# Block 0's first product: wider matmuls for tile pairs, and tile 3 prepared one step sooner

## The chip, the cores and the metric

One core of a Trainium2 chip runs the kernel. The metric is the device time of one execution in microseconds (us); lower is better. Every time below is of the kernel before the change.

## What is computed

Linear attention without a softmax for 8 batches of 8 heads, a norm per head, then a layer norm and a two-layer network with a residual:

```python
kv  = einsum('bhsd,bhse->bhde', k, v)          # q, k, v: (8, 8, 576, 64)
out = einsum('bhsd,bhde->bhse', q, kv)
out = out / sqrt(mean(out*out, -1) + 1e-6) * g_norm
x   = out.transpose(0, 2, 1, 3).reshape(8, 576, 512)
xn  = (x - mean(x)) / sqrt(var(x) + 1e-6) * g_ln
y   = x + maximum(xn @ w_ch1, 0) @ w_ch2       # w_ch1: 512 x 2048, w_ch2: 2048 x 512
```

## The kernel before

**Blocks and tiles.** Each batch gives a block of 512 rows, in four tiles of 128 rows; the 64 rows left of each batch make a ninth block, "rem". Per tile the kernel makes the attention output (`o`), its squares (`sq`, ScalarE), their sums per head (`red`, VectorE), the root of these (`root`, ScalarE, L383), then on VectorE the scaled rows (`y`, L379, and `x`, L397) and the centred, weighted rows in bf16 (`xc`, L407). `turn` transposes these on TensorE (L429) into PSUM, and ScalarE copies them into `xT_blk` (L431), the right operand of the first product.

**First product.** `mm1(b, t0, n, c0, c1)` multiplies tiles t0 to t0+n-1 by the column blocks c0 to c1 of w1 (16 of 128 columns each). One step fills one PSUM bank with 4/n column blocks of n tiles: 16 matmuls 128 columns wide for n = 1, 8 matmuls 256 wide for n = 2, 4 accumulations (`kk`) for each column block. ScalarE then reads the bank in one relu (L678) into `m1`. The banks come from the pool `ps1`, which has three. In blocks 2 to 8 the steps take two or four tiles at once; in blocks 0 and 1 one.

**Second product.** `mm2_part` (L697) multiplies `m1` by w2. For block 0 it starts when all of `mm1(0, ...)` is issued, on two `ps1` and two `ps2` banks.

**Order of the work.** It is written by hand. Each engine runs its instructions in the order in which they are issued. Ahead of each step `mm1` calls `tick()`, which first issues what `at(slot, fn)` has put down for that step, in order of the slot: `at(5.1, before_5)` comes in step 5, behind `at(5, ...)`. Block 0's first product is steps 0 to 15, its second product steps 16 and up. The steps of the kernel before:

| step | products of block 0 | issued ahead of them |
|---|---|---|
| 0 | tile 0, c 0 to 4 | |
| 1 | tile 1, c 0 to 4 | `before_1`: tile 1's transpose, tile 2's `o`, `sq`, `red`, `root`, tile 0's `x_g` |
| 2 | tile 0, c 4 to 8 | `before_2`: tile 2's `o_g`, `x_g`, `xc`; tile 1's `x_g` |
| 3 | tile 1, c 4 to 8 | |
| 4 | tile 0, c 8 to 12 | |
| 5 | tile 1, c 8 to 12 | tile 2's `turn`; `before_5`: all of tile 3 up to `xc` |
| 6 to 8 | tile 2, c 0 to 12 | |
| 9, 10 | tiles 0 and 1, c 12 to 16 | memsets and the loads of batch 2 at step 9 |
| 11 | tile 2, c 12 to 16 | tile 3's `turn` |
| 12 to 15 | tile 3, c 0 to 16 | `q_start` at step 14 |

In block 0 the tiles' `o` have banks of their own: tile 1's in `ps1`, tile 2's in `ps_m`, tile 3's in `ps2` (two banks). `x_g` is the variant of `x` for tiles 0 to 2, which reads a second attention product (`og_ps`) that already holds g_norm.

**Loads.** w1 comes in four pieces of four column blocks (`load_w1`, L115) on POOL's queue, one behind the other, then pieces of w2 (L119) among the loads of batch 1.

Of the kernel before, what the change touches and what calls it, by code (L numbers as in the profile page):

```python
# [14 lines left out]
def kernel(  # L15
# [84 lines left out]
    def load_batches(slot, what, after):  # L100

        def start(i, name, b):
            if i == 0:
                for element in after():
                    nc.gpsimd.tensor_copy(gate, element)
            dst, src = {"k": (k_in, k), "v": (v_in, v), "q": (q_in, q)}[name]
            load(dst[b % NB], src, b)

        for i, (name, b) in enumerate(what):
            at(slot[i] if isinstance(slot, tuple) else slot, lambda i=i, name=name, b=b: start(i, name, b))  # L110
# [325 lines left out]
    def main_tile(b, j, pool=None, tag="ops"):  # L436
        q_t, kvp = qts[b], held[b]
        if b not in blks:
            blks[b] = new_block()
        return Tile([(slice(0, 128), lambda hp: q_t[:, j, hp, :], kvp)], blks[b], j, pool, tag)  # L440
# [32 lines left out]
    def m1_of(b):  # L473
        if b not in m1s:
            m1s[b] = m1pool.tile([128, nDe, 512], bf16, tag="m1", name="m1")
        return m1s[b]
# [22 lines left out]
    def row_sums(b, i0, i1, ticks):  # L499
        if b not in sums:  # L500
            sums[b] = [spool.tile([128, H2, 256], bf16, tag=f"S{i}", name=f"S{i}")
                       for i in (1, 2, 4)]
            sums[b].insert(2, m1_q(b, 1, 0))
        s = slice(i0, i1)
        S1, S2, S3, S4 = (t[:, s] for t in sums[b])
        a11, a12, a21, a22 = (m1_q(b, r, o)[:, s] for r, o in ((0, 0), (0, 1), (1, 0), (1, 1)))
        for i, fn in enumerate((lambda: nc.vector.tensor_add(S1, a21, a22),  # L507
                                lambda: nc.vector.tensor_sub(S2, S1, a11),  # L508
                                lambda: nc.vector.tensor_sub(S4, a12, S2),  # L509
                                lambda: nc.vector.tensor_sub(S3, a11, a21))):  # L510
            agenda.setdefault(clock[0] + ticks[i], []).append((-1, fn))
# [153 lines left out]
    def mm1(b, t0, n, c0=0, c1=nDe):  # L665
        blk, m1 = blks[b], m1_of(b)
        sl = slice(t0 * 128, (t0 + n) * 128)
        per = 4 // n
        for de0 in range(c0, c1, per):
            tick()  # L670
            p1 = ps1.tile([128, per, n * 128], f32, tag="p1", name="p1")
            for i in range(per):
                de = de0 + i
                for kk in range(nK):
                    nc.tensor.matmul(p1[:, i, :], lhsT=w1_sb[:, kk, de * 128:(de + 1) * 128],  # L675
                                     rhs=blk[2][:, kk, sl],
                                     start=(kk == 0), stop=(kk == nK - 1))
            nc.scalar.activation(m1[:, de0:de0 + per, sl], p1, func=AF.Relu)  # L678
            del p1
            if b == 2 and t0 + n == 4 and de0 + per in SPLIT_2:  # L680
                i = SPLIT_2.index(de0 + per)
                row_sums(b, SPLIT_2[i - 1] // 2, SPLIT_2[i] // 2, TICKS_2[i - 1])
            elif b in SEVEN and b != 2 and de0 + 1 in SPLIT:
                i = SPLIT.index(de0 + 1)
                row_sums(b, SPLIT[i - 1] // 2, SPLIT[i] // 2, range(4))
# [62 lines left out]
    def at(slot, fn):  # L748

        i, r = divmod(slot, 32)  # L750
        blocks = [*range(B), "rem"]
        if r > 16 and i < len(blocks) and blocks[int(i)] in SEVEN:
            r = 16 + (r - 16) * 14 / 16
        s = sum(30 if x in SEVEN else 32 for x in blocks[:int(i)]) + r
        agenda.setdefault(int(s + 1e-6), []).append((s, fn))

    def tick():
        for _, fn in sorted(agenda.pop(clock[0], []), key=lambda e: e[0]):
            fn()
        clock[0] += 1  # L760
# [15 lines left out]
    t = [main_tile(0, 0)] + [main_tile(0, i, *((ps1, "p1"), (ps_m, "misc"), (ps2, "p2"))[i - 1])  # L776
                             for i in range(1, 4)]
# [77 lines left out]
        t[2].xc()  # L855
        t[1].x_g()

    def before_5():
        t[3].o()
        t[3].sq()  # L860
        t[3].red()
        t[3].y()
        t[3].x()
        t[3].xc()
# [7 lines left out]
    at(1, before_1)  # L872
    at(2, before_2)
    at(5, lambda: t[2].turn(True))
    at(5.1, before_5)
    at(9.5, next_memsets)
    load_batches(9.6, (("k", 2), ("v", 2), ("q", 2)), lambda: ())
    at(11, lambda: t[3].turn(True))
    for i in range(4):
        at(16 + i, lambda i=i: t[i].var())  # L880
    at(20, lambda: (rstd_of(0), t.clear()))
# [73 lines left out]
        at(40 + i, fn)  # L955


    for ts, c0, c1 in ((0, 0, 4), (1, 0, 4), (0, 4, 8), (1, 4, 8), (0, 8, 12), (1, 8, 12),
                       (2, 0, 12), (0, 12, 16), (1, 12, 16), (2, 12, 16), (3, 0, 16)):
        mm1(0, ts, 1, c0, c1)  # L960
    p2s = [ps1.tile([128, Dm], f32, tag="p1", name="p2") for _ in range(2)]
    p2s += [ps2.tile([128, Dm], f32, tag="p2", name="p2") for _ in range(2)]
    for de0, de1 in ((0, 8), (8, 10), (10, 12)):
# [50 lines left out]
```

## Time and profile before

| | |
|---|---|
| three runs | 279.30, 279.38, 279.63 us; median 279.38 |
| the profiled execution | 279.33 us, of which the span is 277.3 |
| granted TensorE clock | 1.00 |
| TensorE busy | 269.2 us, 97% of the span |
| VectorE, ScalarE, POOL busy | 71%, 65%, 37% |
| block 0's first product | 14.83 to about 32.4 us |

The span is the time from the first to the last instruction; the execution's time has some 2 us more around it. PE is TensorE's matmuls, PEld its weight loads, one for each matmul here, DVE is VectorE, ACT is ScalarE. A share of busy time says how full an engine is on average, not what a stage waits for; an end of a matmul in the profile is modelled, so starts are safer to count from. A wait is put down to what ended last ahead of it; "issue" is time for which the profile shows no releaser.

### The profile page before, as it was taken

The page shows a single profiled execution, that of the slowest core. Times are in us where ns is not written, and L with a number is a line of the kernel's source. Part 1 is how long each engine was busy: PE and PEld are TensorE (multiplying, and loading weights), DVE is VectorE, ACT ScalarE, POOL GpSimd, SP SyncE. Part 2 cuts the span into 40 slices and gives each one's busy share as a digit, 9 for nine tenths or more (in the row PEclk, how much of TensorE's full clock was granted, in tenths as well). Part 3 has the DMA queues.
Part 4 walks back from the last instruction along what each step waited for, and adds up shares of the span by engine and source line. Part 5 has one row for each costly group of instructions (what it writes and reads, how often), then busy time and mean ns, then how long its engine had stood idle before and what let it go on. Part 6 is the DMA issues. An engine that isn't in the chain of part 4 may idle for free.

```text
span 277.3 us, 6629 instructions
## 1 busy us (share of the span) xinstructions
PE 269.2 (97%) x2614; PEld 189.6 (68%) x2614; DVE 195.9 (71%) x446; ACT 179.5 (65%) x398; POOL 101.7 (37%) x127
## 2 busy tenths in 40 slices
PE   8899999999999999999999999999999999999994
PEld 3589855996569886458845874597458745874683
DVE  6676438897966898899569856985797469923564
ACT  3567754796448783777677767776777487846610
POOL 8522770025034256701870187017201800180141
PEclk9999999999999999999999999999999999999999
DMA  7999999959995994995499639991611061105032
GB/s 215 199 207 205 200 197 190 260 106 144 189 183 84 199 126 92 216 227 98 41 185 239 134 26 178 245 134 21 161 28 21 20 163 29 21 20 151 2 76 76
DMA packets 65366, 36.80 MB, mean 133 GB/s; under 512 B 35120, under 2 KB 62004, under 8 KB 65336
## 3 DMA queue, kind: packets, MB, share of 16 engines
q0 software_dynamic: 28736, 18.29, 46.4%
q1 hardware_dynamic: 36008, 17.12, 30.4%
q10 hardware_dynamic: 592, 0.98, 1.0%
q8 instruction: 20, 0.33, 0.5%
q14 instruction: 10, 0.08, 0.1%
HBM read 36.71 MB, written 9.44 MB: 166 GB/s over the span
## 4 chain that ended last, share of the span: by engine, by line
PE 82%; DVE 8%; DMA 4%; ACT 3%; issue 1%; POOL 1%; DVEq 0%; POOLq 0%
PE p L675 42%; PE p L697 8%; PE p_y L519 7%; PE p_z L519 7%; PE p_x L519 6%; PE p_s L519 4%; DMA w_sb<-in_moe_w_ch_dram 4%; PE p_q L519 3%; PE o_ps L298 2%; PE kv_ps L271 2%; DVE S L509 1%; DVE ss L375 1%; DVE x_blk L397 1%; DVE o_ps L379 1%; DVE S L508 1%
## 5 line engine op out<-in xcount | busy, mean ns | idle before, releaser
L675 PE MATMUL p<-xT_blk,w_sb 128*128 128x128 bf16 (+2 forms) x1024 | 131.5, 286 | 0.6 <-DMA w_sb<-in_moe_w_ch_dram 0.4
L678 ACT ACTIVATE m<-p 128x512 bf16<-128x512 f32 x144 | 85.5, 597 | 38.9 <-PE p L675 36.2
L675 PEld LDWEIGHTS <-w_sb 128*128 128x128 bf16 x1024 | 78.7, 98 | 45.0 <-issue 0.7
L519 PEld LDWEIGHTS <-m 128*128 128x128 bf16 x448 | 43.3, 98 | 6.5
L375 DVE TENSOR_REDUCE ss<-sq 128x8 f32<-128x512 f32 x35 | 23.8, 680 | 28.7 <-ACT sq L304 28.6
L582 POOL TENSOR_TENSOR q<-q,x_blk 128x512 f32<-128x512 f32 x6 | 8.1, 1348 | 83.1 <-ACT q L553 83.1
L519 PEld LDWEIGHTS <-S 128*128 128x128 bf16 x344 | 32.8, 98 | 4.8 <-DVE S L509 1.1
L697 PE MATMUL p<-w_sb,m 128*128 128x512 bf16 x128 | 29.6, 379 | 0.0
L415 ACT ACTIVATE dev<-x_blk,st_blk 128x512 f32<-128x512 f32 x36 | 25.8, 718 | 1.4 <-DVE st_blk L401 1.4
L379 DVE TENSOR_TENSOR o_ps<-o_ps,inv 128x512 f32<-128x512 f32 x33 | 23.1, 700 | 3.1
L304 ACT ACTIVATE sq<-o_ps 128x512 f32<-128x512 f32 x35 | 20.8, 595 | 5.0 <-PE o_ps L298 5.0
L397 DVE SCALAR_TENSOR_TENSOR x_blk<-o_ps,g_norm_sb 128x512 f32<-128x512 f32 x33 | 22.8, 691 | 1.1
L519 PE MATMUL p_x<-w_sb,m 128*128 128x256 bf16 x192 | 23.4, 273 | 0.0
L697 PEld LDWEIGHTS <-m 128*128 128x128 bf16 x128 | 12.0, 98 | 12.3
L383 ACT ACTIVATE rms<-ss,eps_sb 128x8 f32<-128x8 f32 x36 | 10.7, 297 | 12.6 <-DVE ss L375 12.2
L507 DVE TENSOR_TENSOR S<-m 128x768 bf16<-128x768 bf16 (+2 forms) x20 | 10.7, 536 | 11.4 <-ACT m L678 11.4
L422 DVE TENSOR_SCALAR xc<-x_blk,st_blk 128x512 bf16<-128x512 f32 x32 | 17.7, 553 | 1.1
L558 DVE SCALAR_TENSOR_TENSOR u<-p_y,rstd,v 128x256 f32<-128x256 f32 x24 | 10.4, 476 | 5.0 <-PE p_y L519 5.0
L509 DVE TENSOR_TENSOR S<-m,S 128x768 bf16<-128x768 bf16 (+2 forms) x20 | 12.6, 634 | 0.4
L553 ACT ACTIVATE v<-p_x,rstd 128x256 f32<-128x256 f32 x24 | 9.4, 475 | 5.0 <-PE p_x L519 5.0
L390 DVE RECIPROCAL inv<-rms 128x8 f32<-128x8 f32 x36 | 7.1, 197 | 7.6 <-ACT rms L383 7.3
L519 PE MATMUL p_z<-w_sb,S 128*128 128x256 bf16 x96 | 11.8, 273 | 0.6 <-DVE S L509 0.6
(143 smaller groups left out, 347.6 us busy)
## 6 DMA issues: line engine op xcount, KB each, us to landing
out_dram<-o_sb SPq DMA_DIRECT2D x24, 256.0 KB, 6.1
w_sb<-in_moe_w_ch_dram POOLq DMA_DIRECT2D x7, 512.0 KB, 13.5
q_in<-in_q_dram POOLq DMA_DIRECT2D x7, 320.0 KB, 5.2
k_in<-in_k_dram POOLq DMA_DIRECT2D x7, 320.0 KB, 7.8
v_in<-in_v_dram POOLq DMA_DIRECT2D x7, 320.0 KB, 11.1
q_in<-in_q_dram POOLq DMA_DIRECT2D x8, 256.0 KB, 8.2
out_dram<-o_sb SPq DMA_DIRECT2D x16, 128.0 KB, 4.6
k_in<-in_k_dram POOLq DMA_DIRECT2D x7, 256.0 KB, 8.7
```

The lines of the kernel that those rows point to most:

```text
L304: nc.scalar.activation(self.sq_t, self.o_ps, func=AF.Square)
L375: nc.vector.tensor_reduce(self.ss, self.sq_t, axis=AX.X, op=ALU.add)
L379: nc.vector.tensor_mul(self.o_ps, self.o_ps, self.inv().to_broadcast([128, H, D]))
L383: nc.scalar.activation(self.r, self.ss, func=AF.Sqrt, scale=1.0 / D, bias=eps_sb)
L397: nc.vector.scalar_tensor_tensor(x_blk[:, ts].rearrange("p (h d) -> p h d", h=H), in0=self.o_ps, scalar=1.0, in1=g_norm_sb.to_broadcast([1 ...
L415: nc.scalar.activation(dev, x_blk[:, ts], func=AF.Square, bias=st[:, 1, ts:ts + 1], accum_out=st[:, 2, ts:ts + 1])
L422: nc.vector.tensor_scalar_add(self.xc_t, x_blk[:, self.ts], st[:, 1, self.ts:self.ts + 1])
L509: lambda: nc.vector.tensor_sub(S4, a12, S2),
L519: nc.tensor.matmul(dst[:, t - ts[0], :c1 - c0], lhsT=a[:, i, t * 128:(t + 1) * 128], rhs=w[:, i, c0:c1], start=start and t == ts[0] and i ...
L675: nc.tensor.matmul(p1[:, i, :], lhsT=w1_sb[:, kk, de * 128:(de + 1) * 128], rhs=blk[2][:, kk, sl], start=(kk == 0), stop=(kk == nK - 1))
L678: nc.scalar.activation(m1[:, de0:de0 + per, sl], p1, func=AF.Relu)
L697: nc.tensor.matmul(p2[:, c0:c1], lhsT=m1s[b][:, de, ts * 128:(ts + 1) * 128], rhs=w2_sb[:, de, c0:c1], start=(de == 0), stop=(de == nDe - 1))
```

## The change

The step list of block 0's first product is regrouped. Tiles 0 and 1 are still taken one by one for c 0 to 4, then together (n = 2) for c 4 to 12 and for c 12 to 16; tiles 2 and 3 are taken together for c 12 to 16. The steps stay 16: tile 0 (step 0), tile 1 (1), tiles 0 and 1 (2 to 5), tile 2 (6 to 8), tiles 0 and 1 (9, 10), tile 3 (11 to 13), tiles 2 and 3 (14, 15). Tile 3's `o`, `sq` and `red` are issued at step 4, not 5, and its `turn` at step 10, not 11.

```diff
-    def before_5():
+    def before_4():
         t[3].o()
         t[3].sq()
         t[3].red()
+
+    def before_5():
         t[3].y()
         t[3].x()
         t[3].xc()
...
     at(5, lambda: t[2].turn(True))
+    at(4, before_4)
     at(5.1, before_5)
     at(9.5, next_memsets)
     load_batches(9.6, (("k", 2), ("v", 2), ("q", 2)), lambda: ())
-    at(11, lambda: t[3].turn(True))
+    at(10, lambda: t[3].turn(True))
...
-    for ts, c0, c1 in ((0, 0, 4), (1, 0, 4), (0, 4, 8), (1, 4, 8), (0, 8, 12), (1, 8, 12),
-                       (2, 0, 12), (0, 12, 16), (1, 12, 16), (2, 12, 16), (3, 0, 16)):
-        mm1(0, ts, 1, c0, c1)
+    for ts, n, c0, c1 in ((0, 1, 0, 4), (1, 1, 0, 4), (0, 2, 4, 12), (2, 1, 0, 12), (0, 2, 12, 16),
+                          (3, 1, 0, 12), (2, 2, 12, 16)):
+        mm1(0, ts, n, c0, c1)
```

## The prediction

> **What bounds the kernel now.** I read the page first, for which engine sets the span. Its columns are busy time, share of the span, count; in the groups, busy and mean ns, then idle time before them and who ended it.
>
> ```profile
> span 277.3 us, 6629 instructions
> PE 269.2 (97%) x2614; PEld 189.6 (68%) x2614; DVE 195.9 (71%) x446; ACT 179.5 (65%) x398; POOL 101.7 (37%) x127
> ...
> L675 PE MATMUL p<-xT_blk,w_sb 128*128 128x128 bf16 (+2 forms) x1024 | 131.5, 286 | 0.6 <-DMA w_sb<-in_moe_w_ch_dram 0.4
> ```
>
> TensorE is the bound, and the groups show almost no idle time ahead of the first products. But a busy matmul is a modelled length that covers the next one's start, so small waits hide in it. The timeline of the weight loads (start, length, count), which come one per matmul, shows them; here block 0's first product:
>
> ```profile
> 18.68 2.80 PEld L675 LDWEIGHTS <-w_sb 128*128 128x128 bf16 x48
> 21.45 0.27 PEld L429 LDWEIGHTS <-xc 128*128 128x128 bf16 x4
> 21.67 0.27 PEld L298 LDWEIGHTS <-qt 128*128 128x128 bf16 x4
> 21.89 2.78 PEld L675 LDWEIGHTS <-w_sb 128*128 128x128 bf16 x49
> 24.87 2.66 PEld L675 LDWEIGHTS <-w_sb 128*128 128x128 bf16 x47 [0.20 <-issue]
> 27.49 0.26 PEld L429 LDWEIGHTS <-xc 128*128 128x128 bf16 x4
> 27.71 0.99 PEld L675 LDWEIGHTS <-w_sb 128*128 128x128 bf16 x17
> 28.87 3.56 PEld L675 LDWEIGHTS <-w_sb 128*128 128x128 bf16 x63 [0.17 <-issue]
> 32.38 0.58 PEld L697 LDWEIGHTS <-m 128*128 128x128 bf16 x4
> ```
>
> From 24.87 to 27.49 there are 47 loads: 55.7 ns each, 0.892 us per step of 16. At that pace the 49 from 21.89 would end at 24.62, not 24.87: 0.25 us lost after the first load of step 8 (49 = 3 x 16 + 1). The 17 from 27.71 would end at 28.66, not 28.87: 0.21 us lost at the start of tile 3, step 12. These are the two waits that the change can touch. A third, of 0.09, lies in the first line (2.77 us for 48 loads, 2.67 at the pace): step 3 goes on when ScalarE's relu of step 1 (19.09 to 19.67) has ended, which the change leaves alone.
>
> Who is waited for: ScalarE's timeline.
>
> ```profile
> 20.81 0.60 ACT L678 ACTIVATE m<-p 128x512 bf16<-128x512 f32 x1 [0.38 <-PE p L675]
> 21.70 0.60 ACT L678 ACTIVATE m<-p 128x512 bf16<-128x512 f32 x1 [0.30 <-PE p L675]
> 22.20 0.58 ACT L431 COPY xT_blk<-tp 128x512 bf16<-128x512 bf16 x1
> 22.66 0.61 ACT L304 ACTIVATE sq<-o_ps 128x512 f32<-128x512 f32 x1
> 24.03 0.30 ACT L383 ACTIVATE rms<-ss,eps_sb 128x8 f32<-128x8 f32 x1 [0.75 <-DVE ss L375]
> 24.24 1.55 ACT L678 ACTIVATE m<-p 128x512 bf16<-128x512 f32 x3
> ...
> 28.24 0.58 ACT L431 COPY xT_blk<-tp 128x512 bf16<-128x512 bf16 x1
> ```
>
> Tile 3's root (L383) stands in ScalarE's order ahead of step 5's relu (L678) and waits 0.75 us for VectorE's sum, which waits for the square at 22.66. Three relus pile up behind it, and step 8 waits for the bank that the first of them gives back near 24.84. At 28.24 the copy of tile 3's transpose ends at 28.82; step 12 goes on at 28.87.
>
> **Wider products.** 64 pairs of 128-column matmuls become 64 of 256 columns: 32 pairs in steps 2 to 5, 16 in steps 9 and 10, 16 in steps 14 and 15. The columns stay the same; only what a matmul costs beyond its columns is saved. Block 2's first product has the wide form, in TensorE's timeline:
>
> ```profile
> 82.25 3.66 PE L675 MATMUL p<-xT_blk,w_sb 128*128 128x256 bf16 x32
> 85.74 0.39 PE L298 MATMUL o_ps<-kv_pack,qt 128*128 128x128 bf16 x4
> ```
>
> 3.49 us for 32 is 109.1 ns, against 2 x 55.7 = 111.5. Saved: 64 x 2.4 ns = 0.15 us, all on the bounding engine. The 64 weight loads that go too were hidden (98 ns each, started every 55.7). The Trainium skill, "TensorE: Matmul & The Clock Gate", section "Back-to-back issue gap", gives about 81 ns for each 128-column matmul in a stream of load and matmul pairs, and 131 ns for 512 columns; interpolated, an estimate from that page, 256 columns would cost some 98 ns and the term would be 64 x 64 ns = 4.1 us. The trace does not agree: 55.7 ns in this very stage.
>
> There are still 16 steps, and each fills one bank that one relu of 512 columns reads (597 ns), so ScalarE's work and every later entry of the agenda keep their step. The second w1 piece is first used at step 2, the third at 4, the last at 9, as before. The step-4 load at 20.56 goes out as the third piece lands (POOL, waiting for that semaphore, goes on at 20.81), so that coming earlier would gain nothing; 0.22 us of tile 3's matmuls now stand ahead of it. Tile 1 is needed from step 1 on in both.
>
> **Tile 3 made a step sooner.** Three instructions move from step 5 to step 4: `o` (4 matmuls on TensorE, ahead of step 4's products), `sq` (ScalarE, ahead of step 4's relu and tile 2's copy) and `red` (VectorE, after tile 1's `x_g`, in the same order as before). No DMA moves, and nothing passes POOL's or SP's queue. I play it through with the rows' spacings (a relu starts 0.25 us after its step's last load, as 21.45 to 21.70; a full ScalarE operation holds its queue 0.50, as 21.70 to 22.20).
>
> Step 3 ends at 20.53 instead of 20.56. `o` loads from 20.53 to 20.75; step 4's eight wide ones end at 21.62; tile 2's transpose at 21.84; step 5 at 22.72, where step 6 wants tile 2's columns. ScalarE: step 3's relu 20.78, `sq` 21.28 to 21.89, step 4's relu 21.87, tile 2's copy 22.37 to 22.95. Before, that copy ended at 22.78, just as step 6 began. So step 6 goes on at 23.0 instead of 22.78: **a new wait of 0.22 us**. Queued behind it is all of TensorE.
>
> In return the sum runs on VectorE at 21.94 (it is free of `x_g` at 21.85 by its timeline) to 22.63; the root comes at 22.83 and waits for nothing, step 5's relu at 23.04 instead of 24.24, and **step 8's wait of 0.25 us goes**. What is late next is tile 2's copy, above.
>
> Tile 3's `xc` ends 3.05 us after its root (24.03 to 27.08 before), so at 25.88. Its transpose, now at step 10, is wanted at about 26.49: covered by 0.6 us. The copy then ends at 27.82, and step 11 goes on at 27.87, wanted at 27.64: 0.23 lost, against 0.21 now. That wait only moves.
>
> **Sum**, against the profiled execution (span 277.3, time 279.33; the 2.0 us around the span stay): -0.15 - 0.25 + 0.22 + 0.02 = -0.16 us, so the second product starts at about 32.22 instead of 32.38. The rest follows TensorE: the next waits (`kv_ps` at 52.73, about 0.2 us; `p_z` at 105.47, 0.58 us idle by TensorE's timeline) are ScalarE's and VectorE's, behind work that TensorE starts, and shift along. The DMA-bound row nearest is VectorE's `q_p` copy at 55.11; tile 3 of block 1, made after it, is ready at 58.30 and transposed at 59.08, so 0.16 us fits into that 0.78. 279.33 - 0.16 = 279.17; the runs' median is 0.05 higher, so **279.2 us**. What a measurement can tell from no change is about 0.2%, 0.56 us (the three runs spread over 0.33): the forecast is no measurable change.
>
> The unknown cost is the new wait at step 6. At best the copy is out before step 6 (as now): 0, sum -0.38. At worst every ScalarE operation holds its queue for its full 0.60: relu 20.78, `sq` 21.38, relu 21.98, copy 22.58 to 23.16, wait 0.43, sum +0.05. I take 0.22, by the spacing of the rows just there.
>
> **Rivals.**
>
> *Both copies come in time.* If step 6 finds tile 2 ready and step 11 finds tile 3 ready, then -0.15 - 0.25 - 0.21 = -0.61 us: 278.8. For: the copy at 22.20 was just in time. Against: one more full operation is ahead of tile 2's copy, and tile 3's is in the same place as at 28.24. Chance 0.20.
>
> *The wide form saves more*, by the 81 ns rule: 275.3. Against: the pace of the loads above. Chance 0.02.
>
> *The gain is given back*: a later product waits for VectorE or a transfer whose time stands still. 279.4, in the margin. Against: the margins above. Chance 0.10.
>
> *Slower: `o` waits for its bank.* Tile 3's `o` writes a bank of the two-bank pool `ps2`, which the turned q of tile 3 (`tp`) and tile 2's `og_ps` held. The trace shows the last readers ending at 18.60 (ScalarE, L846) and 20.22 (VectorE, L365), and only that at 21.67 the load went out unhindered. If the bank is given back later than the readers show, all of TensorE stands from 20.53, up to 21.67: 1.14 us, less the 0.15 and the 0.25, +0.74: 280.1. It decides from a release at about 21.5 on (then over +0.56). Against: 20.22 is 0.3 us early enough. Chance 0.12.
>
> *The change doesn't do what it says*: no. The step lists say which matmuls there are.
>
> **Numbers.** The forecast has 0.52. It and the give-back lie within 0.2%: 0.62. The two copies and the wide form are faster, the bank is slower, and 0.04 stays for what no view shows, half to each side: faster 0.20 + 0.02 + 0.02 = 0.24, slower 0.12 + 0.02 = 0.14. The range goes from the two-copies case with a little scatter, 278.6, past the worst case of the unknown cost (279.4) to a bank given back some 0.9 us late, 279.9; outside are the wide-form case, the fully late bank and part of the unshown. The likeliest case's own range is 279.0 to 279.4.
>
> **What would show it.** Right: loads of step 6 interrupted for 0.2 us near 22.8; none near 24.6; root of tile 3 near 22.8 with no wait for VectorE; one wait of 0.2 us near 27.7; the second product from 32.2; 109 ns per wide matmul. Wrong: a wait ahead of L298 near 20.5 (the bank), a copy L431 that ends before 22.7, or wide matmuls off 109 ns; and if the second product starts as forecast but the end does not follow, the give-back.

## The result, and the profile after

The changed kernel takes 282.12 us (median of 6 runs, 281.44 to 283.77) against 279.51 for the kernel before on the same chip (6 runs, 279.30 to 279.63): ratio 1.0101, 95% interval 1.0083 to 1.0119. It is 2.6 us slower; 279.2 was forecast, at most 279.9. The profiled execution took 281.82. Its page:

```profile
span 279.8 us, 6501 instructions
...
PE 269.9 (96%) x2550; PEld 188.5 (67%) x2550; DVE 195.3 (70%) x446; ACT 180.0 (64%) x398; POOL 101.8 (36%) x127
...
PE 70%; DMA 12%; issue 7%; DVE 6%; ACT 2%; POOL 1%; SPq 0%; DVEq 0%; POOLq 0%
```

There are 64 matmuls and 64 weight loads fewer, as the step list says. The chain of work that ended last, 82% TensorE and 4% DMA before, is now 70% and 12%: transfers set the end in places. Not in block 0, though. Its weight loads in the timeline:

```profile
21.92 0.92 PEld L675 LDWEIGHTS <-w_sb 128*128 128x128 bf16 x9
23.08 3.43 PEld L675 LDWEIGHTS <-w_sb 128*128 128x128 bf16 x55 [0.24 <-issue]
26.52 0.32 PEld L429 LDWEIGHTS <-xc 128*128 128x128 bf16 x4
26.80 0.92 PEld L675 LDWEIGHTS <-w_sb 128*128 128x128 bf16 x9
27.95 4.30 PEld L675 LDWEIGHTS <-w_sb 128*128 128x128 bf16 x63 [0.24 <-issue]
32.27 0.64 PEld L697 LDWEIGHTS <-m 128*128 128x128 bf16 x4
```

The new wait at step 6 (go-on at 23.08), no wait at step 8 (55 loads in one stretch), the wait at step 11, and the second product from 32.27, 0.11 us earlier than before. The loss comes later. Who TensorE's matmuls waited for between 32 and 90 us (total, times, longest; in the kernel before this answer is empty):

```profile
PE o_ps L298 <- DMA qt<-q_p: 1.0, 2, 0.8
PE kv_ps L271 <- DMA v_in<-in_v_dram: 0.7, 1, 0.7
PE tp L429 <- DVE xc L422: 0.5, 1, 0.5
```

Start to start, and less what the matmul ahead takes, these four waits are 0.37 us (at 47.1), 0.63 (59.2), 0.83 (72.8) and 0.93 (83.4): 2.76 us; the text below calls them the four waits. Of two idle stretches of the old trace behind block 0, the one of 0.74 us near 105 is there in both kernels, the one of 0.23 at 52.7 is gone. -0.11 + 2.76 - 0.23 is 2.4, the spans differ by 2.5.

The chain between 40 and 90 us (start, length, what) tells how they hang together:

```profile
33.46 14.20 DMA qt<-q_p
...
62.66 0.74 POOL gate L105
...
64.69 0.70 POOL v_in L97
...
66.69 9.74 DMA q_in<-in_q_dram
...
78.10 6.32 DMA qt<-q_p
...
84.46 0.40 PE o_ps L298 x4
```

Batch 1's q transposes land at 47.66; they landed at 47.02 before, though issued 0.2 us earlier now. Batch 2's q lands 1.5 us later (56.6 for 55.0). VectorE copies it ahead of the rows of block 1's tile 3 (`xc` from 59.35 for 57.81), for which TensorE waits at 59.2. Batch 2's transposes, the gate on POOL's queue that waits for them, batch 3's loads behind the gate, and batch 3's transposes are all late too. TensorE waits at each place where the time in hand was small: 0.37 us at 47.39 in the kernel before, 0.78 at 59.08, 0.9 at 72.4, under 0.1 at 82.0.

Why the first of these transfers is late shows in stretches of 1 us (the last two columns are the busy share of the 16 DMA engines and what they moved, GB/s). After:

```profile
42.00:43.00 1.00, 1.00 (x7) 0.41 (x6) 0.56 (x2) 0.30 (x1) 0.00 (x0) 1.00 1.33 203
43.00:44.00 1.00, 1.00 (x9) 0.61 (x8) 0.94 (x2) 0.15 (x1) 0.00 (x0) 1.00 2.23 174
44.00:45.00 1.00, 1.00 (x7) 0.44 (x5) 0.93 (x4) 0.45 (x1) 0.00 (x0) 1.00 1.28 29
45.00:46.00 1.00, 1.00 (x6) 0.44 (x5) 1.00 (x3) 0.20 (x1) 0.00 (x0) 1.00 1.12 158
```

Before:

```profile
43.00:44.00 1.00, 1.00 (x10) 0.59 (x8) 0.87 (x2) 0.09 (x1) 0.00 (x0) 1.00 1.30 187
44.00:45.00 1.00, 1.00 (x6) 0.42 (x5) 0.93 (x4) 0.51 (x1) 0.00 (x0) 1.00 1.31 185
```

For about a microsecond the transfers nearly stand still, 29 GB/s for 185. In the trace's packets, 32 that began between 43.86 and 44.45 end together at 45.14 to 45.24; packets of their sizes otherwise take about 31 ns (256 bytes) or 69 ns (640 bytes). The queues in the view of transfers, 42 to 46 us, after:

```profile
q0 software_dynamic: 620, 0.39, 88.0%
q1 hardware_dynamic: 620, 0.16, 59.0%
q8 instruction: 1, 0.02, 2.1%
```

and before:

```profile
q0 software_dynamic: 893, 0.53, 90.7%
q1 hardware_dynamic: 855, 0.21, 41.4%
```

q0 are the loads, q1 here the DMA transposes of q in pieces of 256 bytes. New is one packet of the queue "instruction": 16,384 bytes, from 42.93 to 44.25. There are 20 of these in the whole run, in both kernels, on average 249 recorded TensorE instructions apart, so in step with TensorE's instruction count. In the kernel before they came at 34.6, 50.8, 54.6 and 61.1 us, in the changed one at 29.7, 42.9, 55.0 and 58.4. The change takes 128 TensorE instructions away: about half of such a packet. The one at 58.4 meets batch 2's transposes, and the transfers stand again from 59.3 to 60.2. A third, at 82.4, meets batch 3's: the transfers stand from 83.1 to 84.5 (55 GB/s from 83 to 84). These transposes take 6.31 us from issue to landing, 5.05 before, so 1.3 of the 2.4 us by which they land late arise here.

A stand-still need not cost anything: the kernel before has some too, behind its packets at 74.3, 100.7, 131.7, 160.9 and 181.6 for example, and no matmul of it waits for a transfer from 32 us to the end.

### The profile page after: what moved, and what is told of

It is laid out like the page before. It is cut to its first block, busy times and chain, and to the rows that moved or that the text cites. A ratio compares the mean times of both kernels' runs of the same rounds, so it can differ in the third digit from the quotient of the medians.

```text
span 279.8 us, 6501 instructions
## 1 busy us (share of the span) xinstructions
PE 269.9 (96%) x2550; PEld 188.5 (67%) x2550; DVE 195.3 (70%) x446; ACT 180.0 (64%) x398; POOL 101.8 (36%) x127
## 4 chain that ended last, share of the span: by engine, by line
PE 70%; DMA 12%; issue 7%; DVE 6%; ACT 2%; POOL 1%; SPq 0%; DVEq 0%; POOLq 0%
PE p L675 37%; DMA qt<-q_p 7%; PE p_y L519 7%; PE p_z L519 7%; PE p_x L519 6%; PE p_s L519 4%; DMA q_in<-in_q_dram 3%; PE p_q L519 3%; PE o_ps L298 2%; DMA gn_row<-in_g_norm_dram 2%; DVE S L509 1%; PE kv_ps L271 1%; DVE S L508 1%; ACT m L678 1%; DVE q_p L222 1%
## 5 line engine op out<-in xcount | busy, mean ns | idle before, releaser
L675 PEld LDWEIGHTS <-w_sb 128*128 128x128 bf16 x960 | 77.4, 98 | 45.8 <-issue 1.4
L298 PE MATMUL o_ps<-kv_pack,qt 128*128 128x128 bf16 x124 | 12.0, 219 | 1.0 <-DMA qt<-q_p 1.0
L298 PEld LDWEIGHTS <-qt 128*128 128x128 bf16 x124 | 9.2, 98 | 5.4 <-DMA qt<-q_p 1.7
```

What stands on the lines that cost most here:

```text
L298: nc.tensor.matmul(flat[rows, hp * 128:(hp + 1) * 128], lhsT=lhsT_of(hp), rhs=kvp[:, hp, :], start=True, stop=True)
```

## Theory and rivals

**Fetch theory:** TensorE's instructions come in packets of some 250. When a packet comes while DMA transposes are in flight, the transfers stand for about a microsecond. The change moved packets (42.9, 58.4 and 82.4 us) into transposes whose margins are thin. **Rival A:** finishing block 0 some 0.1 us earlier, or tile 3's earlier work, upsets the order of the transfers. **Rival B:** the 256-column products themselves do harm later.

## Experiments

The small matmuls below multiply zeros, and nothing reads them: 64 columns against weights of 128 x 64 by the profile, not the 64 x 64 x 64 that the first expectation names. Each is two TensorE instructions with its weight load. Where they delay TensorE at the start, the delay is read at the second load of step 1 (17.50 us in the changed kernel, 17.43 in the one before). To take such a delay off the total is an estimate: it supposes that the delay reaches the end whole.

**The changed kernel with 128 instructions more.** The tensor `p_pad` is the filling matmuls' bank.

```diff
-    fill(18)
+    p_pad = fill(18)
+    for _ in range(64):
+        nc.tensor.matmul(p_pad[:64, :64], lhsT=fill_sb[:, :64], rhs=fill_sb[:, :64],
+                         start=True, stop=True)
+    del p_pad
```

> The changed kernel with 64 small matmuls (64 x 64 x 64, so 128 TensorE instructions with their weight loads) put into TensorE's idle time before the first k and v rows land (6.6 to 8.3 us). From block 0's first product on, each instruction then has the same number of TensorE instructions ahead of it as in the kernel before. Fetch theory (the 16 KB packets of the instruction queue, one per about 256 TensorE instructions, now fall into the DMA transposes of q at 43 and 58 us, and all transfers stand for 0.8 to 1.3 us): the packets move back to about 34.6, 50.8, 54.6, 61.1, no transfer stands still between 37 and 46, the four waits of TensorE at 47.1, 59.2, 72.8 and 83.4 (2.8 us) go, 279.2 to 279.5 us. Rival A (finishing block 0 some 0.1 to 0.2 us earlier by itself upsets the order of the transfers): still 281.5 to 283.5. Rival B (256-column products write or read something that slows the later transfers): still 281.5 to 283.5.

280.78 us, ratio 1.0039 (1.0023 to 1.0055). The packets come at 34.9, 50.9, 55.1 and 62.1, the transfers do not stand still before 62, q lands at 47.08, and none of the four waits is left. The time still missed the expectation: the small matmuls took 2.2 us, more than the idle time, and put everything off by 0.77. Less that, 280.0; the profiled execution (280.02) less that is 279.25, while other runs went up to 281.1. So by this estimate most of the loss is gone, and a part differs from run to run that the one trace does not show.

**The kernel before with the same 128 instructions more.**

> The kernel before with the same 64 small matmuls in the idle time before 8.3 us; nothing of the change in it. Fetch theory: the packets of the instruction queue move to places half a packet (128 instructions) away from those of the kernel before, which are those of the changed kernel (128 forward and 128 back are the same place modulo 256): a packet at about 42 to 43 and one at about 58 us, in the q transposes; waits of TensorE near 47, 59, 73 and 83 us, 281.4 to 283.8. Rivals A and B: nothing of the change is there, 279.3 to 279.7.

283.72 us, ratio 1.0162 (1.0140 to 1.0184), in the range expected; less its delay of 1.5 us, 282.2. Nothing of the change is in it. A packet at 44.8, a stand-still from 45.5 to 46.8, another at 84.0, waits of 1.13 us at 73.5 and 1.11 at 84.4. The packet expected near 58 came at 61.4, and no wait followed at 47 and 59, since TensorE was late too.

**Control: the changed kernel with 256 instructions more** (13 wide and 133 small ones for `fill(18)`).

> Control for the padding: the changed kernel with 133 small matmuls in place of 5 of the 18 wide ones that fill the time before 8.3 us, so 256 more TensorE instructions. Fetch theory: the same places modulo 256 as in the changed kernel, packets at about 43 and 58 us, 281.4 to 283.8. If it is the small matmuls themselves that help (a warmer or otherwise different start), it would come out at 279.2 to 279.5 as well.

286.92 us, ratio 1.0268 (1.0249 to 1.0287), above what was expected. The start was 4.55 us later; less that, 282.4, the changed kernel's time. Small matmuls as such do not help. The places of the packets relative to the work were not those of the changed kernel, because the transfers did not shift by 4.55: the first came at 47.8, behind batch 1's transposes. The wait of 1.1 us at 88.1 follows a packet at 87.2 and a stand-still from 87.7 to 89.2. Ahead of the one of 1.8 at 76.5 a packet at 64.2 met only the last pieces of batch 2's transposes; these landed 6.5 us after their issue (4.9 in the kernel before), though no other packet was slow. So this control rules out a helpful start more than it confirms a place.

**The order of the change, all products narrow** (as many instructions as before).

```diff
-    for ts, n, c0, c1 in ((0, 1, 0, 4), (1, 1, 0, 4), (0, 2, 4, 12), (2, 1, 0, 12), (0, 2, 12, 16),
-                          (3, 1, 0, 12), (2, 2, 12, 16)):
-        mm1(0, ts, n, c0, c1)
+    for ts, c0, c1 in ((0, 0, 4), (1, 0, 4), (0, 4, 8), (1, 4, 8), (0, 8, 12), (1, 8, 12),
+                       (2, 0, 12), (0, 12, 16), (1, 12, 16), (3, 0, 12), (2, 12, 16), (3, 12, 16)):
+        mm1(0, ts, 1, c0, c1)
```

> The changed kernel's order (tile 3 a step sooner, tile 2's last columns at the end) with all products 128 columns wide, so as many TensorE instructions as in the kernel before. Fetch theory: the packets fall as in the kernel before, no stand-still between 37 and 46, 279.3 to 279.6 (the 0.15 us of the wide form are not gained). Rival A (an earlier tile 3 and another order upset the transfers): 281 or more. Rival B (the wide form is at fault): 279.3 to 279.6 as well.

279.36 us (10 runs, 279.25 to 279.57), ratio 0.9994 (0.9984 to 1.0003): no different from the kernel before. Packets at 34.7, 51.1, 55.3 and 61.1. Tile 3's earlier work and the new order cost nothing, which settles that part of rival A.

**Batch 1's q turned on TensorE, no DMA transposes from 37 to 47.**

```diff
-        nc.sync.dma_start_transpose(
-            qts[1][:, 2:].rearrange("p j hp t -> p (j hp) t"),
-            q_ps[1][:, 2:].rearrange("p j h d -> p (j h d)"))
...
-        turn_q(1, 0, ps_out, "ops")
-        turn_q(1, 1, ps_m, "misc")
+        for j, (pool, tag) in enumerate(((ps_out, "ops"), (ps_m, "misc"), (ps_out, "ops"),
+                                         (ps_m, "misc"), (ps_out, "ops"))):
+            turn_q(1, j, pool, tag)
```

> The changed kernel with batch 1's q turned on TensorE alone: 12 transposes more there (about 0.7 us) and no DMA transpose in flight from 37 to 47 us. The packet of the instruction queue still comes at 40 to 43 us. Fetch theory (a stand-still needs both, the packet and DMA transposes in flight): no stand-still of all 16 queues near 44, no wait for q near 47; the packet near 58 still meets batch 2's transposes. Total about 280.5 to 282: 2.8 us of waits less the first stand-still and what follows from it, plus 0.7. Rival (the packet alone, or something else at that time, holds the transfers): the stand-still near 44 stays, 282.5 to 283.5.

283.13 us, ratio 1.0125 (1.0088 to 1.0162), above what was expected: TensorE waited 1.35 us at 37 for ScalarE's copies of the transposes, which I had not priced. The total alone lies in the rival's range; for the theory the packet matters. It came at 42.7, by itself, and the transfers went on. Stretches and queues (42 to 46 us) of this run:

```profile
43.00:44.00 1.00, 1.00 (x7) 0.44 (x5) 0.23 (x1) 0.60 (x1) 0.00 (x0) 1.00 1.39 187
44.00:45.00 1.00, 1.00 (x6) 0.49 (x5) 0.63 (x2) 0.30 (x1) 0.00 (x0) 1.00 1.40 199
```

```profile
q0 software_dynamic: 1389, 0.78, 138.7%
q8 instruction: 1, 0.02, 1.5%
```

TensorE turns that q itself here, so that a wait for its transposes near 47 was not possible. The next packet met batch 2's transposes at 59.5; the transfers stood from 59.7 to 61.5, and TensorE waited 0.92 us at 83.9.

**32 instructions more.** 19 small matmuls for `fill(3)`.

> The changed kernel with one group of 3 wide filling matmuls replaced by 19 small ones of about the same time, so 32 TensorE instructions more ahead of block 0. Fetch theory: the packet of 43 us comes some 3.5 us earlier, near 39.5, still inside the q transposes (37 to 47); the one of 58 us near 57.5, still at the q transposes of batch 2. A stand-still near 40 and waits as in the changed kernel: 281 to 283.5. If another cause than the place of the packets holds the transfers at 44, the stand-still stays at 44.

281.12 us, ratio 1.0067 (1.0046 to 1.0088). The packet came at 42.2, not 39.5, and the stand-still with it, 43.0 to 44.3: it follows the packet, but 32 instructions more moved the packet by 0.7 us and not by the 3.5 expected. Waits of 0.42 at 47.2, 0.59 at 59.3 and 1.0 at 82.7.

**Half of the wide products** (tiles 0 and 1, c 4 to 12 only).

> The changed kernel with only tiles 0 and 1, c 4 to 12, wide (32 pairs), so 64 TensorE instructions fewer than in the kernel before, where the change has 128 fewer. Fetch theory: the packet that comes at 34.6 in the kernel before and at 42.9 in the changed one comes half-way, near 37 to 38.5, just as the q transposes begin (37); the next near 52 and 56.5, ahead of batch 2's transposes; one near 78, in the transposes of 77 to 82. If the first stays ahead of the transposes: 279.3 to 280; if it falls in: 280.5 to 282.5. Rival B (the wide form itself): half of the loss, about 280.8, whatever the packets do.

280.74 us, ratio 1.0044 (1.0032 to 1.0057). The packet came at 38.0, just inside the transposes, and the transfers stood from 38.8 to 39.8; waits of 0.38 at 47.2 and 0.62 at 59.3, none at 73 and 83. The total alone would fit rival B as well (half of the loss); the place of the stand-still does not.

**The step list alone, tile 3's `o`, `sq`, `red` left at step 5.**

> The changed step list, with tile 3's o, sq and red left at step 5; its transpose is at step 10 as the list asks, where TensorE waits about 0.6 us for its rows. 128 TensorE instructions fewer, as in the changed kernel. Fetch theory: packets in the same places of the program as in the changed kernel, stand-stills near 44 and 58 to 60, 281.5 to 284. Rival A (tile 3's earlier work upsets the order of the transfers): without it 279.6 to 280.2.

282.80 us, ratio 1.0108 (1.0084 to 1.0131). Its own wait of 0.51 at step 10, stand-stills at 44.4, 60.6 and 83.9, waits of 0.42, 2.19 and 1.25 us at 62, 73 and 85. The loss does not need tile 3's earlier work.

**The changed kernel with 128 instructions more at little cost.** With `pads(n, p1)` for n small matmuls:

```diff
-    fill(18)
+    pads(37, fill(14))
...
-    fill(1)
+    pads(6)
...
-    dead = fill(3)
+    dead = pads(19)
...
-    fill(1, dead)
+    pads(6, dead)
...
-    fill(1, dead)
+    pads(6, dead)
```

Ten wide matmuls go (the expectation says 8) and 74 small ones come, so 128 instructions more.

> The changed kernel with 64 matmuls more at no time: in the stretch before block 0's first product, 8 wide filling matmuls (4 of the first 18, 3 and the single ones later) give way to 37 + 6 + 19 + 6 + 6 small ones, at the 33 ns that each took in the first padded run. Same number of TensorE instructions ahead of every later step as in the kernel before, and the first product starts near 14.8 as there. Fetch theory: no waits at 47, 59, 73, 84; the 0.16 us that the first product gains is kept: 279.2 to 279.4, ratio 0.9985 to 1.0005. If the first padded run owed its recovery to TensorE being 0.8 us later (the transfers then having more time), it comes out at 281 or more.

280.02 us (11 runs, 279.70 to 280.13), ratio 1.0019 (1.0010 to 1.0028). No stand-still before 63, no new wait, q on time. The stretch that stood still in the changed kernel:

```profile
44.00:45.00 1.00, 1.00 (x10) 0.53 (x7) 0.93 (x4) 0.60 (x1) 0.00 (x0) 1.00 1.31 185
```

2.1 us of the 2.6 are back, and the runs are close together again. It missed the expectation: TensorE was 0.42 us later at the start after all. Less that it is 279.6, which neither shows nor excludes the 0.16 us.

**The kernel before with the same change of its start.**

> The kernel before with the same 64 matmuls more at no time, nothing else. Fetch theory: half a packet away, so packets near 43 and 58 in the q transposes, waits near 47, 59, 73 and 84 as in the changed kernel: 281.4 to 283.5. If the loss needs something of the change besides its instruction count: 279.3 to 279.6.

282.20 us (281.27 to 283.26), ratio 1.0111 (1.0091 to 1.0131), with a delay of 0.28 at the start: the changed kernel's time, with none of its products and none of its order. Packets at 43.4, 59.3 and 81.0. Of the four waits expected, the trace (of the fastest run, 281.27) has two, 0.53 us at 62.4 and 1.00 at 82.9; q landed at 47.61 and was not late for TensorE. Stretches and queues (42 to 46 us) of this run:

```profile
43.00:44.00 1.00, 1.00 (x10) 0.53 (x8) 0.82 (x2) 0.04 (x1) 0.00 (x0) 1.00 1.32 198
44.00:45.00 1.00, 1.00 (x8) 0.49 (x6) 0.93 (x4) 0.60 (x1) 0.00 (x0) 1.00 2.24 90
45.00:46.00 1.00, 1.00 (x7) 0.45 (x5) 0.96 (x3) 0.00 (x0) 0.00 (x0) 1.00 0.86 117
```

```profile
q1 hardware_dynamic: 654, 0.17, 54.1%
q8 instruction: 1, 0.02, 1.8%
```

Neither rival A nor rival B is needed for the loss, by this run: the instruction count is enough.

**The small matmuls placed better** (45 at the head, then 4, 17, 4 and 4).

> As the run before it (the changed kernel, as many TensorE instructions ahead of each step as before the change), with the small matmuls put where they cost less: that run had TensorE wait 0.5 us for the first v rows at 8.3, and its groups of 6 and 19 were 0.1 us longer each than the wide ones they replaced. Now 45 at the head and 4, 17, 4, 4 later; block 0's first product should start within 0.1 us of 14.8. Fetch theory: packets at 34.6, 50.8, 54.7, 61.2, no new waits, 279.2 to 279.5 (ratio 0.9985 to 1.0005). If the 0.16 us of the first product does not reach the end: 279.4 to 279.7.

279.70 us (279.42 to 280.16), ratio 1.0014 (1.0005 to 1.0023). Packets at 35.0, 51.5, 55.9 and 61.7, no new wait for a transfer. The start was 0.67 us later this time (the filling matmuls took 0.43 us each up to 6.8 us), so the time less the delay is 279.0. The total lies at the end of the second range expected (279.4 to 279.7), so whether the 0.16 us reach the end stays open. No version beat the kernel before: the wide form's gain is smaller than what it cost here to keep the instruction count.

## Why the prediction was wrong

**The steps of block 0 held.** The wide form: the last 63 loads, 47 narrow and 16 wide, took 4.32 us; 47 x 55.7 + 16 x 109.1 ns is 4.36. The wait at step 6 ended at 23.08 (forecast 23.0), step 8's was gone, the root came at 22.91 without waiting for VectorE (22.83), step 11 went on at 27.95 (27.87), and the second product began at 32.27 (32.22); the trace runs 0.07 us late from step 1 on. `o` did not wait for its bank: L298 loaded at 20.55, right behind step 3.

**Two steps failed.** "The 64 weight loads that go too were hidden" priced 128 instructions by their time on TensorE alone; no term stands for the transfers that bring instructions. The 128 were also about half of a packet of the instruction queue, whose lines (20 packets, 0.5% of the DMA engines) were on the page of before, and I took them as nothing. And in "The rest follows TensorE" the transfers were a clock that stands still, so that the margins of 0.78 us and the like could only be used up by TensorE coming earlier. The transfers themselves came later, by 0.6 to 2.4 us, and the thin margins turned that into 2.76 us of waits. The give-back rival had the right place (VectorE and transfers) but supposed transfers "whose time stands still", so it could lose no more than the gain (279.4): I had no cause that makes a transfer later.

**The rivals.** Neither copy came in time, as the forecast said; the 81 ns rule would have shown as narrow loads further apart than 55.7 ns, and they were not; the bank rival fell. The slower side was given 0.14, on a mechanism that did not occur.

**How far the cause is settled.** That the instruction count ahead of the work decides is shown: the old kernel with 128 instructions more becomes as slow as the changed one, the changed order with the old count is as fast as the old kernel, and the changed kernel with the old count gets four fifths of the loss back. A later start alone does not do it: two padded versions of the changed kernel began their first product 0.42 and 0.67 us later and had no such waits. That the packet and the transposes together make the stand-still rests on one direct run, without the transposes, and on a count over the packets of all 13 traces: of 71 such 16 KB packets during which at least 20 pieces of a DMA transpose began, 53 were followed within 0.5 us by a stand-still (10 packets or more of over 0.55 us each); of 192 others, 1 was. The stand-still also moves with the packet: the packets at 38.0, 42.2, 42.9, 43.4, 43.6 and 44.8 us, each in another kernel, were all followed by one 0.8 to 0.9 us after they began. It is a strong tie and no law: 18 of the 71 had no stand-still behind them, and some twenty stand-stills lie elsewhere in the runs. Why the engines stand is open. So is the run-to-run spread (2.3 us in the changed kernel, 0.33 before); transfers that miss or just meet their time would fit it, but no run shows that.

The Trainium skill, "DMA: Bandwidth & Descriptors", section "Rules for kernel authors", says that two DMA transposes from different queues must be serialized, since they can corrupt each other, and that a transpose next to ordinary DMAs needs nothing. That is said of right results, not of time. Beside ordinary loads the traces show no such stand-still (185 GB/s from 44 to 45 us in the kernel before); next to an instruction packet they show a cost in time.

## What to carry to other kernels

Where transfers have little time in hand, count what an edit does to an engine's number of instructions, and look where the packets of the instruction queue fall, before and after; here 128 instructions fewer moved them by about half a packet and cost 1%. When a change is slower in a place that it does not touch, add idle instructions to the old kernel until its count has moved as much: if that alone makes it slow, the loss need not come from what the change computes or in which order. And give DMA transposes that gate a chain of loads more room than the 0.4 us that the first ones had here.

## What the runs showed of the hardware

- A 16 KB packet of the instruction queue came on average every 249 recorded TensorE instructions and took 0.9 to 1.9 us.
- In 53 of 71 cases in which it met DMA transposes, transfers stood for 0.8 to 1.8 us behind it; packets that mostly take under 0.2 us (18 to 41 ns for 256 bytes) then took up to 1.75 us, and ended within 0.31 us of each other.
- Matmuls of 64 columns against 128 x 64 weights ran at 32 ns each, with their weight loads, 37 to 133 in a row.
